# Head transposes of one batch moved from TensorE to DMA, and a new order in the last product

## The chip, the cores and the metric

The kernel runs on one core of one Trainium2 chip. The metric is the device time of one execution in microseconds, the median of several runs. A core has TensorE (PE, with its weight loads listed apart as PEld), VectorE (DVE), ScalarE (ACT), GpSimd (POOL) and SyncE (SP). Transfers are issued from queues of SP, ACT and POOL and are carried by the core's 16 DMA engines.

## The reference

Grouped-query attention, and behind it one residual MLP block with affine scalings in place of norms. Eight batches, 16 query heads on 4 key/value heads, 384 tokens, head size 64, so 1024 channels; inputs and output are float32.

```python
scores = np.matmul(q, k.transpose(0, 1, 3, 2)) / np.sqrt(64)    # k, v repeated to 16 heads
attn = softmax(scores)
x = np.matmul(attn, v)               # heads laid side by side: (8, 384, 1024)
a1 = alpha1 * x + beta1
u = x + lam * einsum('ts,bsd->btd', w_tok, a1)
a2 = alpha2 * u + beta2
out = u + lam * (np.maximum(a2 @ w_ch1, 0.0) @ w_ch2)           # 1024 -> 4096 -> 1024
```

## The kernel before

The two channel products dominate. Batches 0 and 1 are done one at a time in `main(b)`: a first phase of products with w_ch1 (line 531), in 32 blocks of 128 hidden channels, eight matmuls each, and a second phase with w_ch2 (line 569), in six units of 32 matmuls. Batches 2 to 7 are done in three pairs by `pair(i)`, a block algorithm with seven products for eight (line 722 for the first, line 786 for the second product, both over a table of operand sums and of places).

Beside the products of one batch or pair runs the attention and token mixing of the next, the generator `side(b)`: scores and exp (lines 279 and 288), the product with the values (line 315) and its scaling (lines 320 to 330), the token mixing (lines 340 to 351), and the turning of the result to channels on partitions. Where these pieces fall is written out by hand: a product yields after every four matmuls or so, the yields of each phase are counted, and the table `plan` names for a stage, a phase (0 first, 1 second) and a count what is put there. The order of the instructions on each engine and queue is the order in which the Python text emits them (a manual schedule); each engine goes down its own list and waits on semaphores.

What the change and the steps of the prediction touch:

- **Keys and queries turned.** Scores want `kT` and `qT`, head dimension on partitions. Batch 0 is turned on PE, since its inputs come late. For batch 1, `k_transpose` (lines 251 to 257) and `q_transpose` (lines 259 to 267) put six 128x128 transposes on PE for each call, into PSUM, and a DVE copy behind them. For the batches from 2 on, `flip_k` and `flip_q` (lines 171 to 177) issue a transposing transfer from SP, SBUF to SBUF; `put_flips` places one for all keys and four for two pairs of heads each. For batch 1 the calls stand in `turns` (lines 434 to 441), in the first phase of batch 0.
- **Weights.** w_ch1 comes in chunks of 256 hidden channels into a ring of six places, `load_w1` (line 185), w_ch2 in pieces, `load_w2` (line 189). Both are issued from POOL's queue and cast float32 to bfloat16 on the way; a chunk is 512 KB in SBUF. When PE has used a chunk, its place is given to the chunk six further on. In the first phase of batch 0 the chunks end at the sixteenth, and behind them in POOL's queue stand 13 pieces of w_ch2, then the inputs of batch 2.
- **Relus.** A block of the first product in `main` is emptied by a relu on ACT (line 540) or on DVE (line 542). The counter `exps[0]` decides: an exp sets it to 2, each relu takes one off, and a relu goes to ACT when it is below zero. Some exps are put off: `scores(i, later=True)` leaves the exp in the list `late`, and `av` runs it after its own matmuls.
- **Turned rows.** The eight rows of 128 channels of a batch's mixed result are turned by a transfer from SP (`a2_transpose`, line 362, behind the spill of the row to `out`, line 243) or on PE (`turn`, lines 424 to 429, with a copy on ACT). `by_pe` names the rows turned on PE: of the odd batches from 3 on the last three, of batch 1 the last. `sums_a` (lines 586 to 588, DVE) adds the turned rows for the block algorithm.
- **The last product.** In the last pair the product number 4 (line 786, the last of `PLACE2`) is done in two halves `h` of eight hidden blocks, and in each half over the three token tiles `ms`. The third tile's accumulator is in two parts, 384 and 128 columns, in two banks. At the last hidden block each part is scaled, added and sent out (lines 794 to 796).

Of the kernel before, what the change touches and what calls it, by code (L numbers as in the profile page):

```python
# [12 lines left out]
def kernel(  # L13
# [36 lines left out]
    NST = S // P  # L50
# [3 lines left out]
    NP = Hq // 2  # L54
    D1 = D + 1
    NPL = 2
# [151 lines left out]
    late, exps = [], [0]  # L208
# [20 lines left out]
    def side(b):  # L229
# [175 lines left out]
        def av(p):  # L405
            av_piece(p, 0)
            av_piece(p, 1)
            while late:
                late.pop(0)()

        def tok_flip(p):
            tok(p)
            flip(p)
# [5 lines left out]
                a2_transpose(p)  # L419

        def by_pe(p):
            return b % 2 and p >= (NP - 3 if b > NPL else NP - 1)

        def turn(p):
            ps = three()[:, 0].rearrange("p a b -> p (a b)").bitcast(bf)[:, :S].rearrange("p (a b) -> p a b", a=NST)
# [5 lines left out]
        if not first:  # L431


            turns = {}
            if b == 1:
                turns = {5: [(to_all, 3, 0, 0), (load_row_set, 1, 1, 0)], 7: [(to_all, 3, 1, 1), (load_row_set, 2, 0, 1)],
                         9: [(k_transpose, 0)], 12: [(to_all, 1, 0, 2)], 14: [(to_all, 1, 1, 0), (load_row_set, 2, 1, 0)],
                         17: [(scale_beta,)], 20: [(to_all, 2, 0, 1)], 22: [(to_all, 2, 1, 0)],
                         24: [(q_transpose, 0, 2, "av")], 28: [(k_transpose, 2)]}
                for i in range(3):  # L440
                    turns[32 + 4 * i] = [(q_transpose, 2 + 2 * i, 2, "av")]
            if (b - NPL) // 2 > 0:
                at = {}

                def put(k, *m):
                    at.setdefault(k, []).append(m)

                for j in range(6):
                    put((0, 6, 12, 21, 26, 31)[j], scores3, j, j in (2, 5))
                for p in range(NP):  # L450
                    put((4, 10, 14, 18, 24, 29, 33, 35)[p], av, p)
                    put((8, 15, 17, 22, 27, 32, 36, 38 if b % 2 else 39)[p], tok_flip, p)
                    if by_pe(p):
                        put((36, 39, 41)[p - NP + 3], turn, p)
                return turns, at
            return turns, {
                0: [(scores3, 0)], 4: [(av, 0)], 6: [(scores3, 1)], 8: [(tok_flip, 0)], 11: [(av, 1)],
                13: [(scores3, 2, True)], 15: [(av, 2)], 16: [(tok_flip, 1)], 18: [(tok_flip, 2)], 19: [(av, 3)],
                21: [(scores3, 3)], 23: [(tok_flip, 3)], 25: [(av, 4)], 27: [(scores3, 4)], 29: [(tok_flip, 4)],
                31: [(av, 5)], 33: [(scores3, 5, True)], 35: [(av, 6), (tok_flip, 5)], 37: [(av, 7)],  # L460
                38: [(tok_flip, 6)], 41: [(tok_flip, 7)],
                **{39 + 4 * i - i // 2 * 2: [(turn, p)] for i, p in enumerate((5, 6, 7)) if by_pe(p)}}
# [207 lines left out]
    def pair(i):  # L670
# [25 lines left out]
        last = i == NB - 1  # L696
# [12 lines left out]
        for g in range(NH // 2):  # L709
            X, Y, snap = {}, {}, {}  # L710
            for k, (o, e) in enumerate(SEQ1):
                t = 2 * g + e
# [51 lines left out]
        X = [c_banks(ms) if last else None for ms in range(NST)]  # L764
        snap = {}
        where = {2: (0, 0), 3: (0, 1), 7: (1, 1), 4: (1, 0)}
        for k, o in enumerate(PLACE2):
            whole = not last and o != 4
            for h in range(1 if whole else 2):
                for ms in range(NST):  # L770
                    if o == 4 and not last and 1 < 3 * h + ms < 5:
                        sum_w1(0, (5, 7, 6)[3 * h + ms - 2])
                    if last and (o, h) in ((6, 1), (7, 0)):
                        (lift_end if o == 7 else begin_end)(ms)
                    if last and (o, h, ms) == (7, 0, NST - 1):
                        X[ms] = [(c0, c1, pairs[sc].tile([P, 2, 512], f32, tag="sc", name="C", bufs=1)[:, 0, :c1 - c0])
                                 for sc, c0, c1 in (("sc1", 0, 384), ("sc2", 384, 512))]
                    if whole:
                        X[ms] = [(0, 512, acc.tile([P, 512], f32, tag="acc", name="C", bufs=2))]
                    elif not last and h == 0:  # L780
                        X[ms] = c_banks(ms)
                        pairs["held"] = ms == NST - 1
                    upto = NH if whole else 8 * h + 8
                    for (c0, c1, x), t in ((c, t) for c in X[ms] for t in range(8 * h, upto)):
                        slot, rhs = w2_slots[i, 4 * k + t // 4], w2_at[i, 4 * k + t // 4]
                        nc.tensor.matmul(out=x, lhsT=hid[:, t, LEFT2[o], ms * P:(ms + 1) * P],  # L786
                                         rhs=rhs[:, t % 4 * 512 + c0:t % 4 * 512 + c1],
                                         start=((not last or o in (1, 6, 7)) and t == 0), stop=(t == NH - 1),
                                         skip_group_check=True)
                        if t % 4 == 3 and ms == NST - 1 and c1 == 512 and not (o == 4 and slot >= RING):  # L790
                            free(slot)
                        if last and o == 4 and t == NH - 1:
                            e, v = ends[ms][:, c0:c1], spare(ms).bitcast(f32)[:, c0:c1]
                            tt(out=v, in0=x, in1=lam_t[:, c0:c1], op=MUL)
                            tt(out=e, in0=e, in1=v, op=ADD)
                            nc.sync.dma_start(out=by_tok(out[b0 + 1])[:, ms, c0:c1], in_=e)
                        if t % 4 == 3 and t < upto - 1 and c1 == 512:
                            q = 4 * ms + t // 4
                            if whole and o in (2, 6) and q in (2, 5, 8, 10):
                                sums_hid(o, (2, 5, 8, 10).index(q))  # L800
                            if t % 8 == 3 and later and (last or later[0][1] != 4):
                                flush(1)
                            yield 1
                    if k == ms == h == 0:
                        pad_free[:] = [RING + 1, RING + 2, RING]
                        pump()
                    if (whole or h == 1) and not (last and o == 4):
                        if o in (1, 6, 5):
                            q = ((1, 6, 5).index(o) * NST + ms) * 512
                            snap[o, ms] = snaps[:, q:q + 512]  # L810
                        else:
                            bb, dw = where[o]
                            t = snap[1, ms] if o == 7 else spare(ms).bitcast(f32)
                        for c0, c1, x in X[ms]:
                            if o == 1:
                                nc.scalar.copy(out=snap[o, ms], in_=x)
                            elif o in (6, 5):
                                tt(out=snap[o, ms], in0=x, in1=snap[1 if last or o == 6 else 6, ms], op=ADD)
                            elif o == 2 and last:
                                tt(out=t, in0=x, in1=lam_t[:, :512], op=MUL)  # L820
                            else:
                                base = {2: 1, 3: 1 if last else 5, 7: 5, 4: 6}[o]
                                tt(out=t[:, c0:c1], in0=x, in1=snap[base, ms][:, c0:c1], op=ADD)
                            if o == 7 and not last:
                                tt(out=snap[6, ms], in0=x, in1=snap[6, ms], op=ADD)
                        if o not in (1, 6, 5):
                            later.append((scaled, o, b0 + bb, ms, dw, t))
                    if last and o in (2, 6) and (h, ms) in ((0, 1), (0, 2), (1, 0), (1, 1)):
                        sums_hid(o, [(0, 1), (0, 2), (1, 0), (1, 1)].index((h, ms)))
                    yield 1  # L830
# [5 lines left out]
    with tc.manual_schedule(engines=order):  # L836
# [134 lines left out]
        def put_all(ps, phase, table, at=lambda u: u):  # L971
            for u, ms in table.items():
                for m in ms:
                    put(ps, phase, at(u), *m)

        def put_flips(ps, phase, b, places):
            for u, m in zip(places, ((flip_k, b), *((flip_q, b, i, 2) for i in range(0, NP, 2)))):
                put(ps, phase, u, *m)

        turns, at = side(1)  # L980
        put_all(0, 0, turns)
        put_all(0, 1, at)
        put_flips(0, 1, 2, (34, 36, 37, 42, 43))

        put(0, 1, 45, load_next, 3)
# [13 lines left out]
        for i in range(NB - 1):  # L999
            ps, c = NPL + i, NPL + 2 * i + 2  # L1000
# [56 lines left out]
```

## Time and profile before

| | |
|---|---|
| median of 3 runs | 740.31 us (740.12 to 741.42) |
| the profiled execution | 740.56 us |
| its span, first to last instruction | 738.8 us |
| granted TensorE clock, mean | 0.999 |
| PE busy | 731.5 us (99%), 5769 matmuls |
| DVE busy | 516.9 us (70%) |
| ACT busy | 324.1 us (44%) |
| POOL busy | 163.5 us (22%) |
| DMA | 151.32 MB, mean 205 GB/s |
| queue q0 (from POOL) | 120304 packets, 66.6% of 16 engines' span |
| queue q1 (from SP) | 97100 packets, 42.9% of 16 engines' span |
| line 185, loads of w_ch1 | 68 of 512 KB, 10.3 us from issue to landing (median) |
| PE transposes of batch 1, line 255 (keys) and line 265 (queries) | 12 and 24 |

Times in the views count from the first instruction of the span. A row of the timeline has the start, the busy time, the engine and line, the operation, what it writes and reads, shapes, how many instructions are merged, and in brackets the idle time before it and what ended it. A matmul's busy time contains its way through the array: matmuls are pipelined, so the pace is read from one start to the next. The DMA share can go over 1, since an engine has several packets under way. GB/s counts bytes on the SBUF side; a cast load reads twice as many.

### The profile page before, as it was taken

The page shows a single profiled execution, that of the slowest core. Times are in us where ns is not written, and L with a number is a line of the kernel's source. Part 1 is how long each engine was busy: PE and PEld are TensorE (multiplying, and loading weights), DVE is VectorE, ACT ScalarE, POOL GpSimd, SP SyncE. Part 2 cuts the span into 40 slices and gives each one's busy share as a digit, 9 for nine tenths or more (in the row PEclk, how much of TensorE's full clock was granted, in tenths as well). Part 3 has the DMA queues.
Part 4 walks back from the last instruction along what each step waited for, and adds up shares of the span by engine and source line. Part 5 has one row for each costly group of instructions (what it writes and reads, how often), then busy time and mean ns, then how long its engine had stood idle before and what let it go on. Part 6 is the DMA issues. An engine that isn't in the chain of part 4 may idle for free.

```text
span 738.8 us, 14511 instructions
## 1 busy us (share of the span) xinstructions
PE 731.5 (99%) x5769; PEld 418.8 (57%) x5769; DVE 516.9 (70%) x995; ACT 324.1 (44%) x467; POOL 163.5 (22%) x211
## 2 busy tenths in 40 slices
PE   8999999999999999999999999999999999999997
PEld 5866555566555566655555566655555566654444
DVE  7763366467587889749777988847968988762354
ACT  7632431444333566653334366664343266660000
POOL 9434221420000232211013244020002222000011
PEclk9999999999999999999999999999999999999999
DMA  9999999999899999999989999998989999937965
GB/s 184 194 202 200 207 209 175 185 191 199 204 258 281 177 218 212 268 249 205 297 197 197 202 149 191 204 246 198 274 236 172 211 127 145 172 117 261 293 182 103
DMA packets 218017, 151.32 MB, mean 205 GB/s; under 512 B 88660, under 2 KB 197060, under 8 KB 217948
## 3 DMA queue, kind: packets, MB, share of 16 engines
q0 software_dynamic: 120304, 64.60, 66.6%
q1 hardware_dynamic: 97100, 85.39, 42.9%
q8 instruction: 45, 0.74, 0.4%
q10 hardware_dynamic: 544, 0.39, 0.2%
q14 instruction: 24, 0.20, 0.1%
HBM read 154.84 MB, written 38.27 MB: 261 GB/s over the span
## 4 chain that ended last, share of the span: by engine, by line
PE 95%; DVE 2%; DMA 1%; ACT 0%; issue 0%; DVEq 0%
PE C L786 30%; PE X L722 17%; PE h L531 10%; PE ch L569 10%; PE Y L722 8%; PE sc L279 5%; PE Z L722 4%; PE sc L315 4%; PE sc L340 3%; DMA ops<-a 1%; PE h L223 1%; PE tok L340 1%; PE av L315 0%; PE warm L841 0%; PE tp L265 0%; ACT hT L288 0%
## 5 line engine op out<-in xcount | busy, mean ns | idle before, releaser
L288 ACT ACTIVATE es<-sc 128x1024 bf16<-128x1024 f32 x126 | 121.4, 1023 | 155.9 <-PE sc L279 144.8
L786 PE MATMUL C<-w,arena 128*128 128x512 bf16 (+2 forms) x744 | 168.0, 372 | 0.0
L786 PEld LDWEIGHTS <-arena 128*128 128x128 bf16 x1040 | 94.8, 98 | 100.5 <-issue 5.1
L727 ACT ACTIVATE hT<-X,bias 128x384 f32<-128x384 f32 x144 | 83.7, 581 | 61.6 <-PE X L722 54.9
L722 PEld LDWEIGHTS <-w 128*128 128x128 bf16 x768 | 75.1, 98 | 50.0
L516 POOL DMA_DIRECT2D out_dram<-hT x33 | 28.7, 871 | 284.3 <-DVE hT L687 106.3
L569 PE MATMUL ch<-arena,hT 128*128 128x512 bf16 x384 | 90.8, 379 | 0.0
L185 POOL DMA_DIRECT2D w<-in_moe_w_ch_dram x68 | 62.8, 964 | 98.4 <-PE X L722 34.4
L531 PE MATMUL h<-ops,w 128*128 128x384 bf16 (+1 forms) x480 | 83.3, 327 | 0.8 <-DVE hT L542 0.7
L722 PEld LDWEIGHTS <-pad 128*128 128x128 bf16 x576 | 56.4, 98 | 37.2
L722 PE MATMUL X<-ops,w 128*128 128x384 bf16 x384 | 70.2, 326 | 0.0
L722 PE MATMUL X<-ops,pad 128*128 128x384 bf16 x384 | 70.2, 326 | 0.0
L786 PE MATMUL C<-pad,arena 128*128 128x512 bf16 (+2 forms) x296 | 69.9, 373 | 0.0
L531 PEld LDWEIGHTS <-w 128*128 128x128 bf16 x480 | 45.4, 98 | 30.4 <-issue 2.7
L569 PEld LDWEIGHTS <-hT 128*128 128x128 bf16 x384 | 34.8, 98 | 36.8 <-issue 2.5
L347 DVE TENSOR_TENSOR xr<-sc,xr 128x384 f32<-128x384 f32 x56 | 30.9, 552 | 23.4 <-PE sc L340 23.4
L315 PEld LDWEIGHTS <-es 128*128 128x128 bf16 x1008 | 38.2, 97 | 12.4
L340 PEld LDWEIGHTS <-wtokT 128*128 128x128 bf16 x576 | 37.5, 98 | 11.8 <-DVE a L330 0.8
L279 PE MATMUL sc<-qT,kT 64*128 64x384 bf16 (+2 forms) x576 | 42.0, 272 | 0.8 <-DVE xr L323 0.3
L320 DVE RECIPROCAL rinv<-sc 128x6 f32<-128x6 f32 x56 | 10.7, 192 | 44.3 <-PE sc L315 44.1
L315 PE MATMUL sc<-v,es 128*128 128x65 bf16 x1008 | 39.8, 193 | 0.0
L722 PE MATMUL Z<-ops,w 128*128 128x384 bf16 x192 | 39.0, 326 | 0.0
(138 smaller groups left out, 911.0 us busy)
## 6 DMA issues: line engine op xcount, KB each, us to landing
w<-in_moe_w_ch_dram POOLq DMA_DIRECT2D x68, 512.0 KB, 10.3
w<-w2s SPq DMA_DIRECT2D x60, 512.0 KB, 4.3
pad<-w2s SPq DMA_DIRECT2D x24, 512.0 KB, 8.1
out_dram<-xr SPq DMA_DIRECT2D x56, 192.0 KB, 6.1
out_dram<-hT POOLq DMA_DIRECT2D x33, 256.0 KB, 5.7
arena<-in_moe_w_ch_dram POOLq DMA_DIRECT2D x16, 512.0 KB, 20.0
w2s<-arena SPq DMA_DIRECT2D x28, 256.0 KB, 5.0
q_raw<-in_q_dram POOLq DMA_DIRECT2D x28, 192.0 KB, 10.4
```

Source lines behind the costliest of these rows:

```text
L185: nc.gpsimd.dma_start(out=w1[:, w1_slots[c]], in_=w1src[:, :, c * CW * P:(c + 1) * CW * P])
L279: nc.tensor.matmul(out=sc[:, hh, k % 4:k % 4 + n], lhsT=kT[r, 2 * p // G, BLK[hh][sk], :], rhs=qT[r, p, st:st + n, :], start=True, stop=True)
L288: nc.scalar.activation(out=e, in_=sc, func=EXP, scale=scale_qk)
L315: nc.tensor.matmul(out=av[:, hh, sq, :], lhsT=ess[k // 4][:, m % 2, k % 4, :], rhs=vb[:, sk, hk, :], start=(sk == 0), stop=(sk == NST - 1))
L340: nc.tensor.matmul(out=ps[:, tt, :], lhsT=wtokT[:, st, tt * P:(tt + 1) * P], rhs=a1s[p][:, st, :], start=(st == 0), stop=(st == NST - 1 an ...
L347: nc.vector.tensor_tensor(out=u, in0=ps, in1=u, op=ADD)
L516: nc.gpsimd.dma_start(out=at, in_=o, accum_op=ADD)
L531: nc.tensor.matmul(out=ps[:, :n], lhsT=w1[:, w1_slots[c], dt, j * P:(j + 1) * P], rhs=a2T[:, dt, :n], start=(dt == 0), stop=(dt == NDT - 1))
L569: nc.tensor.matmul(out=ps, lhsT=hT[:, nt, ms * P:(ms + 1) * P], rhs=w2[:, row(nt)[0], row(nt)[1], cs], start=(i == 0), stop=(i == NNT - 1))
L722: nc.tensor.matmul(out=ps, lhsT=tb[g, o][:, dt, e * P:(e + 1) * P], rhs=opb(LEFT1[o])[:, dt], start=(o in (1, 2, 7) and dt == 0), stop=(dt ...
L727: nc.scalar.activation(out=snap[o, e], in_=ps, func=IDENT, bias=hi if o == 5 else lo)
L786: nc.tensor.matmul(out=x, lhsT=hid[:, t, LEFT2[o], ms * P:(ms + 1) * P], rhs=rhs[:, t % 4 * 512 + c0:t % 4 * 512 + c1], start=((not last o ...
```

## The change

Four edits. The turning of keys and queries of batch 1 goes from the PE calls in `turns` to `put_flips`, at counts 16, 22, 28, 34 and 40 of the first phase of batch 0. After a deferred exp the counter is set to 1. `by_pe` takes the last two rows in place of three, so row 5 of batches 3, 5 and 7 goes by transfer. In product 4 of the last pair the third token tile is left out of the first half and done whole, all 16 hidden blocks, at the end of the second.

```diff
             while late:
                 late.pop(0)()
+                exps[0] = 1
...
         def by_pe(p):
-            return b % 2 and p >= (NP - 3 if b > NPL else NP - 1)
+            return b % 2 and p >= (NP - 2 if b > NPL else NP - 1)
...
                 turns = {5: [(to_all, 3, 0, 0), (load_row_set, 1, 1, 0)], 7: [(to_all, 3, 1, 1), (load_row_set, 2, 0, 1)],
-                         9: [(k_transpose, 0)], 12: [(to_all, 1, 0, 2)], 14: [(to_all, 1, 1, 0), (load_row_set, 2, 1, 0)],
-                         17: [(scale_beta,)], 20: [(to_all, 2, 0, 1)], 22: [(to_all, 2, 1, 0)],
-                         24: [(q_transpose, 0, 2, "av")], 28: [(k_transpose, 2)]}
-                for i in range(3):
-                    turns[32 + 4 * i] = [(q_transpose, 2 + 2 * i, 2, "av")]
+                         12: [(to_all, 1, 0, 2)], 14: [(to_all, 1, 1, 0), (load_row_set, 2, 1, 0)],
+                         17: [(scale_beta,)], 20: [(to_all, 2, 0, 1)], 22: [(to_all, 2, 1, 0)]}
...
         for k, o in enumerate(PLACE2):
             whole = not last and o != 4
+            tail = last and o == 4
             for h in range(1 if whole else 2):
-                for ms in range(NST):
+                for ms in range(NST - (tail and not h)):
...
-                    for (c0, c1, x), t in ((c, t) for c in X[ms] for t in range(8 * h, upto)):
+                    for (c0, c1, x), t in ((c, t) for c in X[ms]
+                                           for t in range(0 if tail and ms == NST - 1 else 8 * h, upto)):
...
         put_all(0, 0, turns)
         put_all(0, 1, at)
+        put_flips(0, 0, 1, (16, 22, 28, 34, 40))
         put_flips(0, 1, 2, (34, 36, 37, 42, 43))
```

## The prediction

> **What bounds the kernel now.** I read the page's slices first, then the table of stretches, then the timeline of the stage that the diff touches (the first product of batch 0, line 531, some 36 to 75 us), then its transfers. The slices (span cut in 40) show two busy resources, not one: PE and the DMA engines.
>
> ```profile
> PE   8999999999999999999999999999999999999997
> DMA  9999999999899999999989999998989999937965
> ```
>
> The reader is to see that a nine for PE does not make PE the bound: the DMA row has it too. In the table of stretches (us, then busy time per engine, granted clock, DMA share, GB/s) the stage reads:
>
> ```profile
> 60.00:65.00 5.00, 5.00 (x37) 3.12 (x35) 1.89 (x4) 1.48 (x4) 4.00 (x6) 1.00 1.46 198
> ```
>
> PE never idles there and its clock is full, but the DMA share is above one. Which of the two leads is read from one chunk of weights. PE's timeline:
>
> ```profile
> 59.94 2.78 PE L531 MATMUL h<-ops,w 128*128 128x385 bf16 x16
> 62.55 0.50 PE L265 MATMUL tp<-ident,q_raw 128*128 128x128 bf16 x6
> 62.89 12.58 PE L531 MATMUL h<-ops,w 128*128 128x385 bf16 x76
> ```
>
> Sixteen matmuls, one chunk of w_ch1, take 62.55-59.94 = 2.61 us, 0.163 each; six transposes take 62.89-62.55 = 0.34. The last chunk of the stage is the last 16 of the 76, so PE reaches it at 62.89+60x0.163 = 72.7. Its load is the last of line 185 in POOL's timeline, and its landing is told by the view of that line for that instant (us from issue, min/median/max):
>
> ```profile
> 56.47 0.87 POOL L185 DMA_DIRECT2D w<-in_moe_w_ch_dram  x1 [2.07 <-PE h L531]
> 59.41 0.87 POOL L185 DMA_DIRECT2D w<-in_moe_w_ch_dram  x1 [2.08 <-PE h L531]
> ```
> ```profile
> DMA to landing us min/median/max: 11.2/11.2/11.2
> ```
>
> It lands at 59.4+11.2 = 70.6, 2.0 before PE wants it. The one before takes 11.5 and lands at 68.0: chunks land 2.64 us apart, however they were issued, and PE eats one in 2.61. The loads queue behind each other; the transfers, not PE, set the pace, and PE's lead of 2.0 is just what its 36 transposes cost.
>
> **The change, part by part. Heads by transfer.** Removed from PE: six groups of six transposes, 6x0.34 = 2.04 us, and six DVE copies (about 0.56 each, under PE, worth nothing). Added on SP: one transfer of 12 tiles for kT, four of 6 tiles for qT, 36 tiles of 32 KB, 1.18 MB. SP's timeline shows when they go:
>
> ```profile
> 41.34 4.36 SPq L924 DMA_DIRECT2D rows<-in_moe_alpha_dram  x2
> 86.64 0.65 SPq L243 DMA_DIRECT2D out_dram<-xr  x1
> ```
>
> SP is empty from 45.7 to 86.6, their inputs have landed by 35 to 37 and PE has left the old kT and qT, so all five go at once from 45.7, whatever their places in the plan, and nothing on SP stands behind them. They share the DMA engines with the chunks. What a packet of a transpose costs a cast load is in the trace where the two meet: queues with packets and MB, first 82 to 86 us (a load alone), then 94 to 96 (the same kind of load beside a transpose):
>
> ```profile
> q0 software_dynamic: 828, 0.82, 123.7%
> ```
> ```profile
> q0 software_dynamic: 317, 0.32, 93.2%
> q1 hardware_dynamic: 310, 0.07, 29.2%
> ```
>
> Alone the load moves 207 packets per us. Beside 310 packets of 256 B it moves 317 in 2 us, 97 fewer than 414: 0.47 us for 310, or 1.51 ns each. The change has 1.18 MB/256 = 4608 of them: 7.0 us that the weights lose. The lower bound is a transpose alone, at 134 to 135 us:
>
> ```profile
> q1 hardware_dynamic: 1071, 0.27, 129.1%
> ```
>
> 0.93 ns each, 4.3 us. The upper bound is a chunk's own packet, 2.64 us/1024 = 2.6 ns: 11.9 us. I take 7.0, measured in the same mixture.
>
> [...]
>
> PE's gain of 2.04 uses up its lead to the hundredth (72.7-2.04 = 70.66 against 70.6), so the delay passes to PE whole: it leaves the stage 7.0-2.04 = 5.0 later. Behind the chunks in POOL's queue come the pieces of w_ch2 (line 189). The third of them, issued at 61.75, takes
>
> ```profile
> DMA to landing us min/median/max: 16.5/16.5/16.5
> ```
>
> and lands at 78.3; the nineteenth matmul of line 569 wants it, two after
>
> ```profile
> 79.62 1.03 PE L569 MATMUL ch<-arena,hT 128*128 128x512 bf16 x4
> ```
>
> at 80.05. That lead, 1.76, is smaller than 2.04, so 0.28 more is lost. In all 7.0-1.76 = **+5.2 us** (bounds +2.5 and +10.1). Leads further on are larger (the last piece: 83.64 issued, 24.85 to land, wanted at 111.7: 3.2). kT and qT are wanted by the first scores at 76.3, later by then; at packets taken in turn (207 against 155 a us above) 4608 packets need about 20 us and land by 66.
>
> **The tail.** The third tile's 384 and 128 columns end the kernel:
>
> ```profile
> 734.62 0.55 DVE L794 TENSOR_TENSOR hT<-C,vecs 128x384 f32<-128x384 f32 x1
> 735.21 0.56 DVE L795 TENSOR_TENSOR ends<-ends,hT 128x384 f32<-128x384 f32 x1
> 735.68 0.28 DVE L794 TENSOR_TENSOR hT<-C,vecs 128x128 f32<-128x128 f32 x1
> 736.00 0.29 DVE L795 TENSOR_TENSOR ends<-ends,hT 128x128 f32<-128x128 f32 x1
> ```
>
> PE's last matmul ends at 735.0; DVE is late because the wide part came only 8 short matmuls (0.056 each) before. With the whole tile last, 16 short ones follow the wide part: its result is there at 735.0-0.89 = 734.11, and DVE goes 734.15, 734.74, then 735.21 and 735.53 for the narrow part: **-0.47 us** (bounds -0.7, if DVE were wholly free, and 0). The second halves' weights landed by 720, so starting them 1.75 earlier, at 727.9, costs nothing.
>
> **The relu.** After a deferred exp one relu goes to DVE where two did. The view of 180 us, DVE and then PE:
>
> ```profile
> 180.65 0.61 DVE L542 TENSOR_SCALAR hT<-h,bias 128x384 bf16<-128x384 f32 x1
> 181.78 0.61 DVE L542 TENSOR_SCALAR hT<-h,bias 128x384 bf16<-128x384 f32 x1
> ```
> ```profile
> 181.32 1.46 PE L531 MATMUL h<-ops,w 128*128 128x384 bf16 x8 [0.66 <-DVE hT L542]
> ```
>
> PE waits for the first; the diff moves the second to ACT, which is idle. **0** (bounds -1.0, both such waits gone, and +0.2).
>
> **The turned row.** Row 5 of batches 3, 5 and 7 leaves PE (three transposes, 3x0.056 = 0.17, three times: -0.5) for a transfer behind its spill on SP, 384 packets, 0.58 us of the DMA each. The sums of line 586 want it 6 us after its spill in batch 3 (233.4 to 239.75) and 8 in batch 5 (403.8 to 411.96); such transfers land in 4.9 us (median), 9.5 at worst, and in batch 5 two fetches of 512 KB stand before it. What it is late, DVE waits in order: sums, line 823's evictions, then PE's product 6 at 418.2, 0.37 after the last sum. I take +0.5 of waits against -0.5: **0** (bounds -0.5 and +4.8, three times 2 us late less the 0.37).
>
> **Sum.** The profiled execution took 740.56 (span 738.8 and 1.76 around it): 740.56+5.2-0.47 = 745.3. It lies 0.25 above the median, so 745.0.
>
> **Rivals.** (a) Cheap packets: the transposes cost what they do alone, 4.3 us, so +2.5 and -0.47: 742.4. For it: cast loads read twice the bytes they write, transposes do not. Against: the 94 to 96 row. (b) The other side: the load queue gives way without loss, and PE keeps 2.04, the tail 0.47 and the row 0.5: 737.3, faster. This part turns to a gain only where the transposes take under 1.76 us of DMA time, 0.38 ns a packet; the fastest row is 0.93. (c) Dear packets, up to a chunk's own 2.6 ns: +10.1, 749.9; a part of it, 748, if the turns between queues cost more with 512 B packets than with 1 KB ones. (d) Row 5 late in all three places: 747 to 750. [...]
>
> **How the numbers follow.** Forecast 0.57 (its own range 743.3 to 746.8), (a) 0.20, (b) 0.09, (c) 0.08, (d) 0.04, (e) 0.02. The 8-in-10 range leaves out (b), half of (c), (d) and (e), and the lowest sliver of (a): 741.5 to 748. About 0.2% (1.5 us) is what a measurement of this kernel can tell from no change: faster 0.09, within 0.03 (the low end of (a)), slower 0.88.
>
> **What would show it.** Right: PE waits on `w<-in_moe_w_ch_dram` in line 529's matmuls from about 50 us, chunks landing some 4 us apart until about 66, the stage's end near 80.5 instead of 75.5, and the old stall near 181 unchanged. Wrong: PE without gaps there and line 567 starting near 73.4.

## The result, and the profile after

The changed kernel takes 750.11 us (748.75 to 750.87, 5 runs) beside 740.31 (740.07 to 741.42, 5 runs): 1.0127 times as long, interval 1.0114 to 1.014. Measured once more it took 749.34 (749.12 to 750.29, 4 runs), 1.0124 (1.0109 to 1.0138). The forecast was 745.0, with a range up to 748.0: right in sign, and half of the loss. The profiled execution took 749.04 us with a span of 747.3, 8.5 more than before. So the loss is 8.5 where it can be read stage by stage, and 9.0 to 9.8 in the medians.

The loss was placed by the starts of the stages, before and after. In the profile after, the lines of the code between some 440 and 765 count two less; in the experiments they shift by up to ten.

```
first matmul of ...                      before    after    later by
second product of batch 0                 75.30    80.76      5.46
first product of batch 1                 131.00   137.26      6.26
second product of batch 1                187.52   193.04      5.52
first product of pair 0                  243.07   249.20      6.13
first product of pair 1                  416.25   423.72      7.47
first product of pair 2                  589.44   598.38      8.94
last matmul of product 4                 734.78   743.73      8.95
end of the span                          738.8    747.3       8.5
```

Two thirds arise in the first 81 us. Two steps of nearly the same size, 1.34 and 1.47, come in pairs 0 and 1, and the end gives 0.47 back. Between them, comparing the starts of single matmuls, the delay grows by 0.26 near 86 us (the third piece of w_ch2, forecast at 0.28) and by 0.37 near 115 (scores that wait for DVE, row below), falls by 0.54 near 187 (the relu), and grows by 0.78 near 195 (scores that wait for the queries of batch 3, `<-DMA qT<-q_raw`).

```profile
114.79 0.39 PE L279 MATMUL sc<-qT,kT 64*128 64x128 bf16 x4 [0.68 <-DVE xr L323]
```

The idle time in brackets counts from the modelled end of the matmul before. Read from one start to the next, a pause can differ by some tenths; the text says "by the starts" where it uses that reading.

**The first stage.** In the slices PE falls to 6 in slice 4 (56 to 75 us), while the DMA row stays at nine there:

```profile
PE   8996999999999999999999999999999999999998
DMA  9999999999799999999979999997999999937965
```

The table of stretches has the same 5 us as before (us, PE, PEld, DVE, ACT, POOL, clock, DMA share, GB/s):

```profile
60.00:65.00 5.00, 2.89 (x17) 1.48 (x16) 1.36 (x4) 0.74 (x2) 3.11 (x4) 1.00 1.36 183
```

Seventeen matmuls stand where there were 37, at the same full clock. PE's timeline shows why:

```profile
57.31 2.79 PE L529 MATMUL h<-ops,w 128*128 128x385 bf16 x16 [1.50 <-DMA w<-in_moe_w_ch_dram]
61.56 2.79 PE L529 MATMUL h<-ops,w 128*128 128x385 bf16 x16 [1.46 <-DMA w<-in_moe_w_ch_dram]
65.82 2.79 PE L529 MATMUL h<-ops,w 128*128 128x385 bf16 x16 [1.48 <-DMA w<-in_moe_w_ch_dram]
70.08 10.84 PE L529 MATMUL h<-ops,w 128*128 128x385 bf16 x64 [1.48 <-DMA w<-in_moe_w_ch_dram]
80.76 1.03 PE L567 MATMUL ch<-arena,hT 128*128 128x512 bf16 x3
```

Each chunk of sixteen matmuls is followed by a pause until the next one lands, 4.25 us apart where it was 2.64. SP's timeline has the transfers that do this, all issued in one go, and POOL's the last chunk, with its time to landing:

```profile
46.10 3.31 SPq L172 DMA_TRANSPOSE kT<-k  x1
49.51 12.82 SPq L176 DMA_TRANSPOSE qT<-q_raw  x4
```
```profile
60.40 0.87 POOL L185 DMA_DIRECT2D w<-in_moe_w_ch_dram  x1 [3.42 <-PE h L529]
```
```profile
DMA to landing us min/median/max: 17.7/17.7/17.7
```

It lands at 60.4+17.7 = 78.1, before at 70.65: 7.4 later. The view of the queues for 56 to 60 us (packets, MB, share) shows the mixture:

```profile
q0 software_dynamic: 963, 0.49, 87.6%
q1 hardware_dynamic: 957, 0.24, 45.6%
```

The weights move 963/4 = 241 packets a us, one for each packet of a transpose (957/4 = 239); before, alone, they moved 5445 in 14 us (52 to 66), 389 a us. So 239 transpose packets cost 1-241/389 = 0.38 us, 1.59 ns each; over 4608 packets that is 7.3 us.

**The relu.** Around 186 us, DVE and ACT, then PE:

```profile
186.21 0.58 ACT L538 ACTIVATE hT<-h,bias 128x384 bf16<-128x384 f32 x1 [1.61 <-PE h L529]
186.70 0.61 DVE L540 TENSOR_SCALAR hT<-h,bias 128x384 bf16<-128x384 f32 x1
```
```profile
186.84 1.46 PE L529 MATMUL h<-ops,w 128*128 128x384 bf16 x8
```

PE goes on at 186.84, right behind the relu that is now on ACT. It had waited 0.66 us for the same one on DVE (0.82 by the starts, 0.28 now).

**The turned rows.** Pairs 0 and 1 have a pause of PE that was not there. DVE and PE in pair 0:

```profile
415.37 0.55 DVE L347 TENSOR_TENSOR xr<-sc,xr 128x384 f32<-128x384 f32 x1
```
```profile
415.98 1.02 PE L786 MATMUL C<-pad,arena 128*128 128x512 bf16 x4 [1.35 <-DVE xr L347]
```

Pair 1 has the same at 590.64; by the starts each pause is 1.5. The matmuls that wait begin the third token tile of product 4; DVE's operation reads the PSUM result of row 6's token mixing. In the kernel before the same tile begins without a pause at 408.50, with the fifth of the eight matmuls below. What it waits for there is ACT's emptying of row 5, just turned on PE, which is done at 407.81, in time:

```profile
407.33 0.48 ACT L429 COPY ops<-sc 128x384 bf16<-128x384 bf16 x1 [2.47 <-PE sc L427]
407.64 1.89 PE L786 MATMUL C<-pad,arena 128*128 128x512 bf16 x8
```

The pause ends with DVE and not with a transfer, so this is not the late transfer of the forecast.

**The tail.** The last four DVE operations:

```profile
743.09 0.56 DVE L794 TENSOR_TENSOR hT<-C,vecs 128x384 f32<-128x384 f32 x1 [1.18 <-PE C L786]
743.68 0.56 DVE L795 TENSOR_TENSOR ends<-ends,hT 128x384 f32<-128x384 f32 x1
744.16 0.28 DVE L794 TENSOR_TENSOR hT<-C,vecs 128x128 f32<-128x128 f32 x1
744.48 0.29 DVE L795 TENSOR_TENSOR ends<-ends,hT 128x128 f32<-128x128 f32 x1
```

From the last matmul's start to the last sum's start it is 744.48-743.73 = 0.75 us, before 736.00-734.78 = 1.22: 0.47 less.

### The profile page after: what moved, and what is told of

Its sections match the earlier page's. It is cut to its first block, busy times and chain, and to the rows that moved or that the text cites. A ratio compares the mean times of both kernels' runs of the same rounds, so it can differ in the third digit from the quotient of the medians.

```text
span 747.3 us, 14373 instructions
## 1 busy us (share of the span) xinstructions
PE 726.8 (97%) x5665; PEld 415.3 (56%) x5724; DVE 512.4 (69%) x987; ACT 324.0 (43%) x466; POOL 163.7 (22%) x211
## 4 chain that ended last, share of the span: by engine, by line
PE 82%; DMA 8%; DVE 5%; POOL 3%; issue 3%; SPq 0%; POOLq 0%
PE C L786 26%; PE X L720 17%; PE ch L567 10%; PE Y L720 8%; PE h L529 4%; PE sc L279 4%; PE Z L720 4%; PE sc L315 4%; PE sc L340 3%; DMA arena<-in_moe_w_ch_dram 3%; DMA q_raw<-in_q_dram 2%; DMA w<-in_moe_w_ch_dram 2%; POOL w L185 1%; DVE xr L323 1%; DVE a1f L328 1%
## 5 line engine op out<-in xcount | busy, mean ns | idle before, releaser
L786 PE MATMUL C<-w,arena 128*128 128x512 bf16 (+2 forms) x711 | 163.7, 372 | 1.6 <-issue 0.3
L567 PE MATMUL ch<-arena,hT 128*128 128x512 bf16 x366 | 87.7, 379 | 1.1 <-issue 0.3
L720 PE MATMUL Y<-ops,w 128*128 128x384 bf16 x192 | 39.2, 326 | 0.0
```

Of the source, the lines that this page charges most:

```text
L567: nc.tensor.matmul(out=ps, lhsT=hT[:, nt, ms * P:(ms + 1) * P], rhs=w2[:, row(nt)[0], row(nt)[1], cs], start=(i == 0), stop=(i == NNT - 1))
L720: nc.tensor.matmul(out=ps, lhsT=tb[g, o][:, dt, e * P:(e + 1) * P], rhs=opb(LEFT1[o])[:, dt], start=(o in (1, 2, 7) and dt == 0), stop=(dt ...
```

## The experiments

All medians stand beside 740.2 to 740.3 us of the kernel before, run with them on the same chip.

```
kernel                us (lowest-highest, runs)       ratio, 95% interval
tail_relu             739.65 (738.92-740.59, 11)      0.9991 [0.9982, 0.9999]
tail_relu_k3_behind   740.17 (739.08-742.27, 11)      0.9998 [0.9989, 1.0007]
best_of_parts         741.62 (740.23-744.19, 11)      1.0018 [1.0009, 1.0027]
heads_on_te           743.25 (741.86-746.17, 6)       1.0047 [1.0031, 1.0063]
row5_only             743.61 (743.34-744.68, 5)       1.0045 [1.0033, 1.0058]
queries_only          745.99 (745.10-748.31, 6)       1.0079 [1.0066, 1.0091]
keys_only             746.23 (745.97-748.72, 5)       1.0088 [1.0075, 1.0101]
heads_copied          746.65 (744.99-746.79, 5)       1.0079 [1.0065, 1.0092]
row5_turn_kept        746.68 (746.52-749.22, 5)       1.0086 [1.0073, 1.0099]
heads_k3_behind       747.59 (745.61-749.58, 6)       1.0101 [1.0084, 1.0118]
heads_only            747.70 (746.90-749.09, 4)       1.0100 [1.0085, 1.0114]
row5_on_te            747.95 (747.03-749.64, 4)       1.0106 [1.0093, 1.0119]
changed_again         749.34 (749.12-750.29, 4)       1.0124 [1.0109, 1.0138]
queries_late          749.72 (749.29-750.88, 4)       1.0127 [1.0114, 1.0141]
queries_held          750.00 (748.20-753.33, 5)       1.0140 [1.0123, 1.0157]
```

### The turned row: bank or transfer

The three shared banks of a pair, sc0 to sc2, are handed out in turn by `three()`, also to scores, values and token mixing. The third token tile of product 4 always takes sc0 (`c_banks`). A turning on PE that is left out is one request fewer, and all requests behind it move by one bank. Here the turn is moved on without a request:

```diff
+    def skip_bank():
+        pairs["turn"] = (pairs["turn"] + 1 + (pairs["turn"] == 2 and pairs["held"])) % 3
...
                 for p in range(NP):
...
+                    if b % 2 and p == NP - 3:
+                        put(36, skip_bank)
```

> The changed kernel, row 5 still by transfer in batches 3, 5 and 7, but in batches 5 and 7 the turn among the three shared PSUM banks moves on by one where the turning of row 5 took a bank before. Bank theory (with one bank request fewer, the PSUM result of row 6's token product falls into the bank that the third tile of product 4 takes next, and PE waits until DVE has read it): both stalls of 1.35 us ended by <-DVE xr on the product-4 line are gone, first product of pair 1 comes 6.1 us later than in the kernel before and that of pair 2 too (now 7.5 and 8.9), span 747.3-2.8 = 744.5, median about 747. Late-transfer theory (the sums of row 5 wait for its DMA, as my forecast had it): the transfer is unchanged, so the span stays at 747.3.

The two pauses on the product-4 line are gone and the median falls by 2.7 to 3.4 us (746.68 beside 749.34 and 750.11), with the transfers of row 5 as they were. The profiled execution does not show the fall, though: its span is 747.4, the longest of its five runs. Part of that is in its pairs: product 6 of the next pair now pauses for 1.25 and 0.51 us by the starts, at 425 and 600, as in best_of_parts below; and near 141 PE waits 1.43 for row 6 of batch 1. The pauses settle that it was the bank; its size is better read from the kernels that follow.

```diff
-            return b % 2 and p >= (NP - 2 if b > NPL else NP - 1)
+            return b % 2 and p >= (NP - 3 if b > NPL else NP - 1)
```

> The changed kernel with row 5 of batches 3, 5 and 7 turned on TensorE again, as in the kernel before. Both theories of the row (bank, late transfer) give 747.3-2.8 = 744.5 for the span; the bank theory alone says that this is the same as with the bank turn kept. If PE's own time for the nine transposes matters (3x0.17 = 0.5 us), this one is 0.5 above that run.

747.95, no pause on the product-4 line. The span of the profiled execution is 747.9, not the 744.5 expected, since PE waits elsewhere: 1.52 near 140 (row 6 of batch 1), 0.69 near 196 (queries of batch 3), 0.55 and 0.90 near 460 (a late chunk of w_ch1, see below). The median is 1.3 above the run with the bank turn kept, with overlapping intervals: no more can be said of the difference.

The row alone, in the kernel before (the same edit the other way round):

> The kernel before with row 5 of batches 3, 5 and 7 by transfer and nothing else. Bank theory: two pauses of 1.5 us on the product-4 line ended by <-DVE xr, nothing before pair 0: +2.7, median 743.0; the wait of the row-5 sums is hidden behind these pauses. With heads on TensorE in all else this must equal the step from the tail-and-relu kernel (739.65) to the changed kernel with heads on TensorE (743.25): +3.6 at most. If the row cost nothing with the heads left alone, 740.3.

743.61, +3.4 (interval +2.4 to +4.3). Its profile has both pauses, 1.52 and 1.51 by the starts, and no other new one; pair 1 begins 0.85 later and pair 2 2.39. The span grows by 2.7 (738.8 to 741.5), somewhat less than the two pauses; pair 0 began 0.5 earlier in this execution than in that of the kernel before.

### All good parts together

Tail and relu alone, on the kernel before:

> The kernel before with only the tail and the relu changed: heads and row 5 on TensorE. Tail: -0.47. Relu: my forecast said 0; the theory now, from the stall near 181 that was 0.82 us and became 0.28 in the changed kernel, is that the relu that moved to ACT is the one PE waited for: -0.5. Span 738.8-1.0 = 737.8 by this, 738.3 if the smaller stall came only from the shift of that stage; PE's pause near 180.5 is 0.3 by the one, 0.8 by the other.

739.65: faster, by 0.1 to 1.3 us. The pause near 181 is 0.28 by the starts, so it was the moved relu that PE waited for. The profiled span is 738.8 all the same: in that execution PE stands still near 40 us and is 1.40 late at the second product of batch 0, before anything that was changed.

Then row 5 by transfer with the bank turn kept (`skip_bank` as above):

> The kernel before with the tail, the relu, and row 5 by transfer with the bank turn kept; heads on TensorE. Bank theory: row 5 by transfer is then free and saves PE up to nine transposes of 0.056 us, 0.5: median 739.65-0.5 = 739.1, no stall on the product-4 line. If the transfer of row 5 costs something by itself (its DMA late, the fetches pushed back), 740 to 741.

741.62, and so 2 us worse than tail and relu without it: the 739.1 that I expected fell. There is no pause on the product-4 line, but two new ones in product 6 of the next pair. DVE and PE, in pair 1's beginning:

```profile
412.75 0.56 DVE L592 TENSOR_TENSOR ops<-ops 128x768 bf16<-128x768 bf16 x1 [1.53 <-DMA ops<-obuf]
```
```profile
418.41 0.32 PE L728 MATMUL Y<-ops,w 128*128 128x384 bf16 x1 [1.01 <-DVE ops L593]
```

DVE's sums (line 584 in the changed kernel) wait 1.53 for the transfer of row 5, issued at 403.03 and there at 412.7, and 5.7 us later PE waits for the last of the sums behind it. Pair 2's beginning has 0.69 of the same. So the late transfer of the forecast exists. In the changed kernel DVE waits for it too (1.32 near 420), but PE has lost its 1.5 us at the bank by then, and the sums come in time: the one wait hides the other. (row5_turn_kept agrees: without the bank's pause PE loses time there, 1.25 at 425.)

### The heads: the price by dose

Heads on TensorE again, all else as changed:

> The changed kernel with the heads of batch 1 turned on TensorE again: tail, relu and row 5 as changed. If the heads cost what the stage marks say (first product of the second stage 5.5 us later, 6.1 by the first pair with the relu's half us taken off), the span is 747.3-6.1 to -6.7 = 740.6 to 741.2, median about 743; the two stalls of 1.35 us on the product-4 line stay. If my smaller price (5.2) were right and the rest of the loss lay elsewhere, 742.1.

743.25, as the stage marks said, and 6.1 to 6.9 below the changed kernel. The profiled execution is one of its two longest (745.46, span 743.6): there PE waits 0.52, 0.47 and 1.13 for chunks of w_ch1 between 163 and 173 us. The two bank pauses stay (1.51 each by the starts). (The edit is the heads' part of the change, reversed.)

Keys alone by transfer (12 of 36 tiles; the diff against the changed kernel is shown), queries alone (24; the other way round), and the heads alone on the kernel before (36):

```diff
-        put_flips(0, 0, 1, (16, 22, 28, 34, 40))
+        put(0, 0, 16, flip_k, 1)
...
+                         24: [(q_transpose, 0, 2, "av")]}
+                for i in range(3):
+                    turns[32 + 4 * i] = [(q_transpose, 2 + 2 * i, 2, "av")]
```

> The changed kernel with only the keys of batch 1 by transfer (12 of 36 tiles, 1536 packets), the queries on TensorE. Lead theory: 1536x1.58 ns = 2.4 us of delay to the weights, of which the lead of the second stage's weights takes 1.76: +0.7 over the kernel with all heads on TensorE (743.25), about 743.9. If the loss were in proportion to the tiles (a third of 6.9), 745.5.

> The changed kernel with only the queries of batch 1 by transfer (24 of 36 tiles, 3072 packets), the keys on TensorE. Lead theory: 3072x1.58 ns = 4.85 us, less 1.76: +3.1 over 743.25, so 746.3, up to 1 more where row 6 of batch 1 is late too. In proportion to the tiles: +4.6, 747.8. If the keys' transfer alone made the loss (the first and largest, in front of the others), 743.3.

> The kernel before with the heads of batch 1 by transfer and nothing else. Lead theory: first matmul of the second product of batch 0 5.5 us later (7.3 of transfers less 1.76 of lead). With what comes behind (row 6 of batch 1 late near 138 us, up to 1.7; queries of batch 3 late near 194, up to 0.9) the whole is 5.5 to 8: median 746 to 748. The relu stall must still be 0.8 us (near 187), as this edit does not touch it; 0.3 would say that the heads moved it away. Without tail and relu it stands 1.0 above the sum of the changed kernel's own parts.

The lead of a transfer is the time between its landing and the moment when it is wanted. At the place where most of the price is paid the lead theory, delay = packets x 1.58 ns - 1.76, comes out (1.58 was worked out from the changed kernel, so the row of 36 is no test of it; the rows of 12 and 24 are):

```
tiles by transfer   packets   expected   second product of batch 0 later by
12 (keys)             1536      +0.67     +0.64
24 (queries)          3072      +3.1      +3.18
36                    4608      +5.5      +5.42 (heads_only), +5.46 and +5.76 (changed)
```

Four more profiles with all 36 by transfer have +4.95 to +6.00 here, and the kernels with the heads on TensorE lie between -0.57 and +0.17 (tail_relu, with its pause near 40, apart). So one profile tells this delay to about half a us; a delay in proportion to the tiles, +1.8 for the keys, is outside that, while for the queries, +3.6, it is not.

Of the medians, the queries' follows within its interval, +2.7 over heads_on_te where 3.1 was expected; the keys' does not, +3.0 for 0.7. The profile of keys_only shows two more places of this kernel that are short of time. Near 135 PE waits 1.4 for row 6 of batch 1. Near 457, in the first product of pair 1, it waits 0.8 for DVE, which had stood 2.32 for a chunk of w_ch1 (`<-DMA w<-in_moe_w_ch_dram`). In the kernel before DVE stands 1.62 at that chunk and PE loses nothing; where DVE stands 2 us or more, as here and in row5_on_te (3.11), heads_copied (2.41) and queries_held (2.07), PE loses 0.6 to 1.5. The wait for row 6 in row5_on_te:

```profile
140.38 0.81 PE L529 MATMUL h<-ops,w 128*128 128x384 bf16 x4 [1.52 <-DMA ops<-a]
```

In heads_only the relu's pause near 187 is 0.82 by the starts as before, which shows that the heads did not move it. DVE and PE there:

```profile
186.59 0.61 DVE L539 TENSOR_SCALAR hT<-h,bias 128x384 bf16<-128x384 f32 x1
```
```profile
187.26 1.46 PE L528 MATMUL h<-ops,w 128*128 128x384 bf16 x8 [0.66 <-DVE hT L539]
```

### What of a transpose costs: bytes, packets or the turning

The five transfers as plain copies, against the changed kernel (`copy_k` is written like `copy_q`):

```diff
-        put_flips(0, 0, 1, (16, 22, 28, 34, 40))
+        put(0, 0, 16, copy_k)
+        for u, i in zip((22, 28, 34, 40), range(0, NP, 2)):
+            put(0, 0, u, copy_q, i)
...
+    def copy_q(i):
+        nc.sync.dma_start(out=qT[:, i:i + 2].rearrange("p a j s -> p (a j s)"),
+                          in_=qrs[1][:, 2 * i:2 * (i + 2)].rearrange("p h st d -> p (h st d)"))
```

> The changed kernel with the five transfers of the heads as plain copies of the same 1.18 MB to the same places: keys and queries are not turned, so the attention of batch 1 is computed from unturned tiles. If the price of the heads goes by bytes (the engines move 1.18 MB beside the loads, whatever the form), the first matmul of the second product is late by 5.5 us as in the changed kernel, median 749.5. If it goes by packets (a plain copy moves the same in fewer, longer packets than 4608 of 256 B): at half the packets 3.6-1.76 = 1.9 late, median about 746. If the turning itself is what costs, near 0, 743.3.

The stage ends 1.44 later, neither the 5.5 of bytes nor the 0 of the turning, and the median is 746.65. The same 1.18 MB go in 640 packets of 1.5 and 3 KB, by the shapes (five transfers of 128 partitions; in the rows below 547 packets are 0.88 MB, 1.6 KB each in the mean). The queues at 50 to 54 us:

```profile
q1 hardware_dynamic: 547, 0.88, 69.2%
q0 software_dynamic: 555, 0.28, 50.5%
```

Again as many packets of one queue as of the other, but long ones on q1. The last chunk lands at 74.07, 3.4 later than before, where the transposes made it 7.4: the copy takes 3.4 us for 1.18 MB from the loads, 345 GB/s, the transposes 160. The rows above say the same: the loads moved 555 packets in 4 us where alone, at 389 a us, they move 1556, so 0.88 MB of the copy cost 1001/389 = 2.57 us, 342 GB/s. So the price goes neither by bytes (7.4 for both) nor by the number of packets alone (640 at 1.59 ns would be 1.0): by these two figures a packet costs more when it is longer, but less than in proportion. The copy has longer packets and does not turn, both at once. How much of the difference is the turning itself was not tried; a copy in packets of 256 B would tell.

### Can a later place hide the heads?

Two of the four transfers of queries placed in the second product of batch 0 (against the changed kernel):

```diff
-        put_flips(0, 0, 1, (16, 22, 28, 34, 40))
+        put_flips(0, 0, 1, (16, 22, 28))
+        put(0, 1, 1, flip_q, 1, 4, 2)
+        put(0, 1, 3, flip_q, 1, 6, 2)
```

> The changed kernel with the last two transfers of queries (12 of 36 tiles) issued in the second stage of batch 0, some 80 us, and not in the first. Lead theory: the first stage ends only 4.85-1.76 = 3.1 us late (5.5 to 6.0 now); the 2.4 us moved meet the weights of the second stage, whose last piece has 1.4 us of lead left, and lose 1.0 there: span some 1.4 us less than the changed kernel, median about 748.2, if the late queries are there when the scores want them. If each tile costs the same wherever it goes, no change: 749.5; if the queries come too late for the scores near 100 us, a wait <-DMA qT<-q_raw there and more than 749.5.

749.72, and a first stage as late as ever (+5.38). The experiment did not do what it was meant to: SP had nothing else in its queue and issued the two at 55.4 and 58.7, where the changed kernel has them at 56.0 and 59.3. A place in the plan is an order, not a time. On ScalarE's queue they are held (`flip_q` takes the queue as its last argument):

```diff
-        put_flips(0, 0, 1, (16, 22, 28, 34, 40))
+        put_flips(0, 0, 1, (16, 22, 28))
+        put(0, 1, 1, flip_q, 1, 4, 2, nc.scalar)
+        put(0, 1, 3, flip_q, 1, 6, 2, nc.scalar)
```

> The changed kernel with the last two transfers of queries issued by ScalarE in the second stage of batch 0, some 80 us, where its queue holds them behind its other work. Lead theory, as for queries_late: first matmul of the second product only 3.1 us late (24 tiles), then 1.0 more as the moved 2.4 us meet the weights' last lead of 1.4; whole some 1.4 below the changed kernel (749.5): 748.1. If each tile costs the same wherever it goes, 749.5; if the queries come late for the scores near 100 us or ScalarE's issuing delays the exps, above 749.5.

750.00. The first stage now ends 2.61 late (3.1 expected), but by the end of the second all is lost again, and more: +7.01. ACT's queue and PE:

```profile
79.91 1.31 ACTq L176 DMA_TRANSPOSE qT<-q_raw  x1
81.26 2.65 ACTq L176 DMA_TRANSPOSE qT<-q_raw  x1
```
```profile
118.72 1.46 PE L567 MATMUL ch<-arena,hT 128*128 128x512 bf16 x6 [2.05 <-DMA arena<-in_moe_w_ch_dram]
```

PE waits 2.05 for the last piece of w_ch2, which lands at 118.67 (116.58 in the changed kernel), and 1.97 near 113.5 for a row behind a late transfer (DVE waited 3.78 until the transfer had read a buffer that it was to write). The lead of 1.4 that I had worked out was too large. What the first stage gained by the move the second lost: the transfers were paid where they went.

### The rest of the heads' price

Batch 3's keys are loaded by POOL just when SP issues row 6 of batch 1, near 134 us. Here their loads stand behind those of the queries:

```diff
-        for a in range(2):
+        for a in range(0 if b == 3 else 2):
             yield nc.gpsimd.dma_start, dict(out=k2s[b][:, :, a], in_=by_head(k[b]))
...
+        for a in range(2 if b == 3 else 0):
+            yield nc.gpsimd.dma_start, dict(out=k2s[b][:, :, a], in_=by_head(k[b]))
```

> The kernel row5_on_te (heads by transfer, tail and relu as changed, row 5 on TensorE; 747.95) with the loads of batch 3's keys queued behind those of its queries, so that they leave some 143 us and not 133. If the wait near 138 us on <-DMA ops<-a comes from the collision with that load, it is gone, and the median is 1.0 to 1.6 lower: 746.4 to 747. If row 6 is late by itself, the wait stays, 748.

> The kernel with only the tail and the relu changed (739.65), and the loads of batch 3's keys behind those of its queries. With the heads on TensorE row 6 of batch 1 has its lead, so nothing changes: 739.6, unless the keys now come too late for their own turning near 160 us, which would show as a wait on kT and 740 or more.

In the profiled execution of heads_k3_behind the wait near 138 is gone: row 6 lands 2.7 us after its issue, where it took 4.3 to 6.4 in the changed kernel and its relatives, and this execution takes 745.61. But the six runs fall into two groups, 745.6 to 746.3 and 748.9 to 749.6, and the median, 747.59, is not below that of row5_on_te (747.95) by more than their spread. The control did not change measurably (740.17 beside 739.65). And the changed kernel, once more and unedited:

> The changed kernel once more, unedited, for a second profiled execution and more times. Late-row theory: the heads' transfers also push batch 2's loads some 7 us back, into the transfer of row 6 of batch 1 that PE wants near 138.5 us; in some executions (two of the three with the heads by transfer that were profiled so far, 1.6 to 1.7 us each, not the first) PE waits there on <-DMA ops<-a, so the spread is wide, 748.5 to 751, and its middle lies about 1 us over the first profiled execution (749.06). If there is no such wait in executions of this kernel, the first profile is typical and the median is 749.0.

749.34, with next to no wait near 138 in its profile either (0.06; row 6 took 5.2): the late row is not in every execution, and not the whole reason for the spread. That row 6 lands sooner with the keys' loads out of its way is seen in one profile, which is no proof that they alone delayed it. What makes the other executions 3 us longer is open, since none of them was profiled; chunks of w_ch1 that land late, as near 457 above and near 170 in heads_on_te, are one candidate.

## Why the prediction was wrong

**Heads: the mechanism right, the size, 5.2, too small.** That the weights set the pace, that each transposed packet takes time from them, and that the loss is what is left after the lead: shown at three doses, to within half a us. Pauses for `w<-in_moe_w_ch_dram`, chunks 4.25 apart and a stage end of 80.76 came nearly as written (the pauses from 55 to 70 us, where 50 to 66 was forecast). The 7.0 us measured 7.3 to 7.4. That this price carried over was in part luck: the row of 94 to 96 us has loads in packets of 1 KB, the stage has packets of 0.5 KB, and 1.51 and 1.59 ns need not have been alike. Read strictly, the first matmul of the second product waits for the last chunk, 7.4 late with a lead of 2.0 (5.4; measured 5.46), and only the third piece of w_ch2 brings in the lead of 1.76 (measured 5.72 near 86 us, where the forecast had 5.2). What failed is the end of that step, where I took the later leads as large enough and added nothing behind the stage: "Leads further on are larger" looked only at w_ch2. In the changed kernel's profile scores then wait for DVE (0.37 near 115) and for the queries of batch 3 (0.78 near 195); in six of its relatives PE waits 0.3 to 1.5 for row 6 of batch 1, which goes by SP's queue and had next to no lead: in the kernel before PE takes it with an idle 0.04. The changed kernel's two profiles have no such wait. The heads alone cost 6.3 in the profiled execution and 7.5 in the median (interval 6.3 to 8.4); where the rest of the median's price lies is not shown.

**The turned row: the step that failed.** "What it is late, DVE waits in order ... I take +0.5 of waits against -0.5: 0" had the right kind of wait and overlooked another. A transpose on PE is also a request for a PSUM bank, and leaving it out turned the rotation so that product 4 asked for the bank that was read last. The forecast had 0 for this row; it cost +2.7 in spans, +3.4 in the median (row5_only), within the bounds of -0.5 and +4.8, but by a mechanism that none of the rivals had. Rival (d), the late row, is real as well, 1.0 and 0.7 of PE's time in best_of_parts, yet shows only where the bank is put right; that kernel is 2 us slower than tail_relu.

**The relu: wrong by half a microsecond.** "PE waits for the first; the diff moves the second" was read from two rows. Three relus in a row stood on DVE before, the first at 176.5; the change moved the one in the middle, and that is the one PE waited for. Measured -0.54 at its place, within the bounds; the sign "the old stall near 181 unchanged" did not come.

**The tail: right**, -0.47 expected, -0.47 by the starts and in the span.

**The sum.** Heads +7.5, row +3.4, tail and relu -0.6, each alone: 10.3, where the whole is 9.0 to 9.8 (the intervals of each term are about 1 wide to either side). The forecast had 5.2, 0 and -0.47. Of the 4 to 5 us that were missing, some 3 are the bank and 2 the heads (in the changed kernel's profile 0.5 of it in the first stage and some 1.0 in later waits). Rival (c), 749.9, comes closest in time, and for the wrong reason: a packet cost 1.6 ns, not 2.6.

The lowest median here is tail_relu's, 739.65, which leaves heads and row 5 on TensorE.

## What to carry to other kernels

An operation that is taken away also gives back its turn in whatever is handed out in rotation; before costing it, count the requests on from there and see who now meets whom. In a stage where loads arrive just in time, a transfer that relieves an engine can be a loss: here it saved PE 2.0 us and took 7.4 from the loads. Its price is not told by its bytes: the same 1.18 MB took 7.4 us in 4608 packets and 3.4 in 640. A second wait can stand behind the first, so the gain of removing one is not the length of its pause.

## What the runs showed of the hardware

Beside cast loads a transpose from SBUF to SBUF takes 1.59 ns of the loads' time for each packet of 256 B, 160 GB/s (the changed kernel, 56 to 60 us); a plain copy of the same bytes took 5.3 ns for each of 640 packets (3.4 us), 345 GB/s (heads_copied). Two queues that both had work moved nearly the same number of packets (963 and 957 in 4 us, 555 and 547 in 4 us), so the one with the shorter packets got the smaller share of the bytes (0.24 MB beside 0.49, 0.28 beside 0.88). And some kernels differ from one execution to the next far more than others: 748.2 to 753.3 us (queries_held), 741.9 to 746.2 (heads_on_te), 740.2 to 744.2 (best_of_parts) and 745.6 to 749.6 (heads_k3_behind) beside 738.9 to 740.6 (tail_relu). Profiles of several of them show PE or DVE waiting for a transfer that lands just when it is wanted; that this is the reason was not tried.
